# Gradient of a gated MLP beside an FFT convolution: gradient-row products queued behind the convolution's VectorE operation, one more idle slot ahead of the paired tiles, convolution stores held during four-bank products

## The chip, the core and the metric

The kernel runs on one core of a Trainium2 chip, in bf16 with f32 accumulation in PSUM. The metric is the device time of one execution in microseconds (us). Three runs of the kernel before gave 1858.02, 1858.46 and 1858.56, so the median is 1858.46. A profile was taken of one more execution. Its own time is 1857.48, and the span between its first and last recorded instruction is 1855.7; every time on the trace's axis counts from the start of that span.

## The reference

What has to be computed is the forward output and the nine gradients of

```python
xn = _layernorm(x, axis=-1)                      # x = A_q, [1, 2048, 1024]
return x + _A_ref(xn, A_k, A_v, shift_k, ssm_k, ssm_D) + _B_ref(xn, W_gate, W_up, W_down)
# A: kv = shift4(k) * v ; y = fftconv(kv, ssm_k) + kv * ssm_D ; result xn * y
# B: gate = xn @ W_gate ; up = xn @ W_up ; h = gate * (gate > 0) * up ; result h @ W_down
_out, _vjp = jax.vjp(_f, A_q, A_k, A_v, A_shift_k, A_ssm_k, A_ssm_D, B_W_gate, B_W_up, B_W_down)
```

with 2048 rows, 1024 columns and a hidden width of 3584. B_x is not used. So there is an MLP with three weight matrices, and its backward pass, and a long convolution with its backward pass.

## The kernel before, in words

**The MLP's phases.** Class LnMlp issues the large products, all of them as matmuls of 128x128 weights against 512 columns, eight to a group (`gemm8`) or sixteen (`gemm16`). `hidden` (L1121, 0 to about 631 us) has 14 blocks of 8 row tiles. A block does for each row tile a gate group (PSUM tile ps_g), an up group (ps_u) and a gradient-row group (ps_h, `grad_row`, L1301). ScalarE (ACT) evicts ps_h as gh (L1305), and VectorE (DVE) multiplies the row's pair ru by gh in place (L1306). VectorE also makes ru's second half out of ps_u (L1177) and the product ht (L1183). The stores of ht and ru (L1190, L1311) go to DRAM scratch h_d and ug_d; `defer` and `tick` issue them two steps late. `grad_down` (L1445, to about 846 us, ps_d) and `grad_in` (L1484, to 1272 us, ps_w) make the weight gradients. Both have a form called `four` (L1405) which works on four PSUM banks at once while its operands still arrive: once at the start and once at the end of `grad_down`, and once at the start of `grad_in`. The row tiles xn_nat are loaded (L1092) during the second of these, through its callback `freed`, and its successor uses them at L1413. `out_phase` (L1532, 1272 to 1460 us, ps_o) makes h @ W_down, and `grad_x` (L1648, ps_x) the gradient of x.

**The convolution.** Class ABranch does the FFT as small matmuls (PSUM tile ps_c, L83), evictions by ScalarE (L87), products and block transposes ("flips", `flip`, L341) on VectorE, for eight groups of 128 channels. It is a generator, `slots` (L691), which yields pairs: a block of matmuls or None, and a VectorE function or None. `steps` (L585) runs one pair at each turn: matmuls first, then the VectorE operation, then `stores` (L108), then at most one group of loads from a queue. A store is put on a list by `store` (L105) and issued by the third `stores` after it. The spectral product of a group begins with `f2_pair`, eight pieces that read what the flips of the last slots of the group before have written.

**Who sets the order.** The order on each engine is the program's own. The MLP's phases yield nanoseconds each time they have issued about eight matmuls (1730), and the loop at the end runs the convolution's next slot as soon as enough has gone by: 1900 for a slot with `hidden`; 1900 or, for a slot without matmuls, 1250 in the later phases, which are called dense. So a slot is a place between two groups of eight MLP matmuls, and what comes earlier in the code stands earlier in each engine's queue.

```python
    a_steps, left = a.steps(), A_START
            for ns in phase:
                left -= ns
                while a_steps is not None and left <= 0:
                    d = next(a_steps, None)
...
                        pri.strict = False
                        b.open_right(B_W_down)
                    else:
                        left += d
```

When the convolution has ended, its memory is released, the order is no longer held (`strict` is False; it became True when the convolution's slots began), and `open_right` (L1516) issues four loads of 1.75 MB each (L1522), which bring W_down for `out_phase` as tile wd: rows kt 0 to 6, 7 to 13, 14 to 20 and 21 to 27. They stand on the queue of SyncE (SP), which issues nearly all DMAs, in its program order. wd lies where convolution buffers lay, so its first load waits for their last reader, the store of gh to gh_d.

While `four` runs, `cap` is 2 instead of 3: the convolution may then use two PSUM banks in a block, and larger blocks are split into parts (`parts`, L545) that run one after the other.

Of the kernel before, what the change touches and what calls it, by code (L numbers as in the profile page):

```python
# [48 lines left out]
class ABranch:  # L49
# [58 lines left out]
    def stores(self):  # L108
        for o in self.out:
            o[0] -= 1  # L110
        while self.out and self.out[0][0] <= 0:
            _, out, in_ = self.out.pop(0)
            self.pri.late()
            self.pri.pin(self.nc.sync.dma_start(out=out, in_=in_))
# [576 lines left out]
    def slots(self, st, gi):  # L691
# [148 lines left out]
        yield None, flG  # L840
        yield None, None
        yield None, None

A_START = 60_000


class LnMlp:
# [273 lines left out]
    def hidden(self, first, goT, load, ln, tables, Wg, Wu, Wd, g, xn_d, h_d, ug_d):  # L1121
# [6 lines left out]
        for n in range(N):  # L1128
# [135 lines left out]
            def last_rows(sp):  # L1264

                self.hold = True
                for q in range(2):
                    load_down(sp // 2 + q)

                def run(f, s):  # L1270
                    f(s)
                    yield from step(self.PACE[f is up])
                yield from run(gate, sp)
                yield from run(gate, sp + 1)
                yield from run(up, sp)
                yield from run(gate, sp + 2)
                yield from run(gate, sp + 3)
                load_gate()
                yield from run(up, sp + 1)
                yield from grad_row(sp)  # L1280
                yield from run(up, sp + 2)
                yield from run(up, sp + 3)
                load_up()
                if n == 1:
                    chunk()
                if swap:
                    next_rows(sp)
                    next_rows(sp + 2)
                for s in range(sp + 1, HS):
                    yield from grad_row(s)  # L1290
                if swap:
                    next_grads(sp)
                    next_grads(sp + 2)
# [7 lines left out]
            def grad_row(s, after={}):  # L1301
                ps = self.ps_tile("ps_h")
                self.gemm8(ps, gT[s], wd, None, after)
                gh = self.e1_tile("gh")
                self.pri.pin(nc.scalar.copy(out=gh[:], in_=ps[:]))  # L1305
                self.pri.pin(nc.vector.tensor_tensor(out=ru[s][:], in0=ru[s][:], in1=gh[:].rearrange(  # L1306
                    "p (o f) -> p o f", o=1).to_broadcast([P, 2, 512]), op=ALU.mult))

                def store(r=(s0 + s) * P, cols=cols, t=ru[s]):
                    queue = nc.gpsimd if n == 0 and s < 2 else nc.sync  # L1310
                    self.pri.pin(queue.dma_start(out=ug_d[r:r + P, :, cols], in_=t[:]))  # L1311
                self.defer(store)
                yield 1730
                self.tick()

            def next_grads(sp):
# [6 lines left out]
            def grad(sp):  # L1323
                for s in (sp, sp + 1):
                    at = 3 if sp == 0 else 0
                    yield from grad_row(s, {at: lambda: flip_ahead(sp)} if ahead and s == sp + 1 else {})
                if swap:
                    next_grads(sp)
# [512 lines left out]
```

## Time and profile before

| | |
|---|---|
| median of three runs | 1858.46 us |
| profiled execution: its time, its span | 1857.48, 1855.7 us |
| instructions recorded | 32102 |
| VectorE, ScalarE, GpSimd busy | 60%, 35%, 1% of the span |
| TensorE matmuls in ps_w, ps_d (L1397) | 381.1 and 169.8 us, 379 ns each |
| convolution evictions (L87, 128x512) | 576, 293.9 us, 611 ns each |
| flips (L341) | 96, 180.3 us, 1933 ns each |
| DMA | 344.64 MB, mean 186 GB/s |
| granted TensorE clock | 9 of 10 or more in all 40 slices; 1.00 for the core |

PE is TensorE's matmuls, PEld its weight loads, DVE VectorE, ACT ScalarE, POOL GpSimd, SP SyncE and SPq SyncE's queue of DMA issues. Matmuls are pipelined: one of 512 columns shows 379 ns, but the next one starts about 216 ns after it. So the distance from start to start, rather than the busy time, tells where TensorE lost time. In a timeline a row is its start, the time to its end, the engine, the line, the operation, out<-in, the count, and in brackets the idle time just before it with what ended it. In a table of waits the three numbers are the total, the number of times and the longest.

### The profile page before, as it was taken

The numbers are of one execution on the slowest core, as the hardware profiler recorded it, in microseconds if no ns is written. First come the engines' busy times: TensorE is split into PE (matmuls) and PEld (weight loads), VectorE is DVE, ScalarE is ACT, GpSimd is POOL, SyncE is SP. The second block draws the span as 40 slices with busy tenths as digits, with TensorE's granted clock in tenths as the row PEclk, the third lists the DMA queues.
The fourth block names the chain that finished last, engine by engine and source line by source line (L and its number), as shares of the span: only waits on it lengthen the run. The fifth ranks groups of instructions, "written<-read, shape, count | busy, mean of one in ns | idle before, by whom it ended". The sixth has DMA issues, their size and how long they took to land.

```text
span 1855.7 us, 32102 instructions
## 1 busy us (share of the span) xinstructions
PE 1848.7 (100%) x13061; PEld 847.5 (46%) x13061; DVE 1114.7 (60%) x1634; ACT 646.4 (35%) x1215; POOL 22.6 (1%) x59
## 2 busy tenths in 40 slices
PE   9999999999999999999999999999999999999999
PEld 4444444444444444444444444444444544444444
DVE  6646797797789758584786676721122222466652
ACT  5644444544444454544545555330000000111100
POOL 1000000000000000000000000000000000000000
PEclk9999999999999999999999999999999999999999
DMA  9897669968757856549657444469999857799973
GB/s 269 243 215 191 155 174 235 223 153 205 173 156 197 254 158 165 140 123 257 150 138 177 134 136 126 139 176 292 238 252 250 195 144 166 175 209 212 200 159 74
DMA packets 747876, 344.64 MB, mean 186 GB/s; under 512 B 575832, under 2 KB 715088, under 8 KB 747728
## 3 DMA queue, kind: packets, MB, share of 16 engines
q1 hardware_dynamic: 736592, 320.30, 71.9%
q10 hardware_dynamic: 9504, 17.04, 3.1%
q0 software_dynamic: 1632, 5.24, 0.8%
q8 instruction: 102, 1.67, 0.4%
q14 instruction: 46, 0.38, 0.1%
HBM read 143.79 MB, written 103.83 MB: 133 GB/s over the span
## 4 chain that ended last, share of the span: by engine, by line
PE 71%; DVE 2%; DMA 1%; SPq 0%; issue 0%; DVEq 0%
PE ps_x L1693 21%; PE ps_w L1397 20%; PE ps_o L1561 10%; PE ps_d L1397 8%; PE ps_c L83 3%; PE ps_u L1062 2%; PE ps_h L1062 2%; PE ps_g L1062 2%; PE ps_d L1413 1%; DVE t L91 1%; PE ps_r L1595 0%; PE ps_w L1413 0%; DMA xn_nat<-xn_d 0%; DMA vt<-in_A_v_dram 0%; DVE u L91 0%; DVE arena L91 0%
## 5 line engine op out<-in xcount | busy, mean ns | idle before, releaser
L1397 PE MATMUL ps_w<-ugs,xn_nat 128*128 128x512 bf16 x1728 | 381.1, 379 | 0.0
L87 ACT CAST arena<-ps_c 128x512 bf16<-128x512 f32 x576 | 293.9, 611 | 82.5 <-PE ps_c L83 82.3
L1062 PEld LDWEIGHTS <-xnT 128*128 128x128 bf16 x1792 | 171.8, 98 | 208.8 <-issue 5.4
L341 DVE STREAM_TRANSPOSE arena<-arena 128x1024 f32<-128x1024 f32 x96 | 180.3, 1933 | 135.5 <-ACT arena L87 114.3
L1397 PEld LDWEIGHTS <-xn_nat 128*128 128x128 bf16 x1728 | 165.3, 98 | 201.1 <-issue 6.7
L1062 PE MATMUL ps_u<-wu,xnT 128*128 128x512 bf16 x896 | 206.0, 379 | 0.0
L1062 PE MATMUL ps_g<-wg,xnT 128*128 128x512 bf16 x896 | 205.2, 379 | 0.4 <-DVE xnT L1106 0.3
L1062 PE MATMUL ps_h<-wdT,goT 128*128 128x512 bf16 x896 | 204.1, 379 | 0.0
L1693 PE MATMUL ps_x<-wgT,ggT 128*128 128x512 bf16 x896 | 198.6, 379 | 0.0
L1693 PE MATMUL ps_x<-wuT,guT 128*128 128x512 bf16 x896 | 198.6, 379 | 0.0
L1711 ACT ACTIVATE w<-xn,m 128x512 f32<-128x512 bf16 x32 | 24.3, 807 | 479.5 <-DVE m L1704 366.1
L1561 PE MATMUL ps_o<-wd,hT 128*128 128x512 bf16 (+1 forms) x896 | 187.6, 372 | 0.0
L1397 PE MATMUL ps_d<-g_nat,hs 128*128 128x512 bf16 x768 | 169.8, 379 | 0.0
L1305 ACT CAST gh<-ps_h 128x512 bf16<-128x512 f32 x112 | 66.2, 591 | 201.6 <-PE ps_h L1062 188.8
L1693 PEld LDWEIGHTS <-guT 128*128 128x128 bf16 x896 | 87.7, 98 | 105.7
L1693 PEld LDWEIGHTS <-ggT 128*128 128x128 bf16 x896 | 87.7, 98 | 105.5
L1062 PEld LDWEIGHTS <-goT 128*128 128x128 bf16 x896 | 86.5, 98 | 104.1 <-issue 1.4
L1561 PEld LDWEIGHTS <-hT 128*128 128x128 bf16 x896 | 87.7, 98 | 100.0
L1400 ACT CAST wi<-ps_w 128x512 bf16<-128x512 f32 x108 | 64.6, 599 | 189.0 <-PE ps_w L1397 151.9
L1177 DVE SCALAR_TENSOR_TENSOR ru<-ru,ps_u 128x512 bf16<-128x512 bf16 x112 | 76.4, 683 | 83.6 <-PE ps_u L1062 43.2
L1553 DVE TENSOR_TENSOR ya<-ya,xe 128x1024 bf16<-128x1024 bf16 x16 | 11.1, 693 | 173.2 <-DMA xe<-xn_d 173.2
L91 DVE TENSOR_TENSOR t<-arena 128x2048 bf16<-128x2048 bf16 x96 | 114.1, 1219 | 0.5
(145 smaller groups left out, 1401.9 us busy)
## 6 DMA issues: line engine op xcount, KB each, us to landing
ugs<-ug_d SPq DMA_DIRECT2D x112, 256.0 KB, 5.0
ug_d<-ru SPq DMA_DIRECT2D x110, 256.0 KB, 3.3
wg<-in_B_W_gate_dram SPq DMA_DIRECT2D x56, 256.0 KB, 4.3
wu<-in_B_W_up_dram SPq DMA_DIRECT2D x56, 256.0 KB, 4.7
hs<-h_d SPq DMA_DIRECT2D x56, 256.0 KB, 4.1
out_dram<-wi SPq DMA_DIRECT2D x56, 256.0 KB, 3.9
h_d<-ht SPq DMA_DIRECT2D x108, 128.0 KB, 1.9
gt<-in_grad_out_dram SPq DMA_DIRECT2D x32, 256.0 KB, 5.7
```

What stands on the lines that cost most here:

```text
L83: self.pri.pin(self.nc.tensor.matmul(out, lhsT=lhsT, rhs=rhs, start=start, stop=stop))
L87: self.pri.pin(self.nc.scalar.copy(out=out, in_=in_))
L91: self.pri.pin(self.nc.vector.tensor_tensor(out=out, in0=in0, in1=in1, op=op))
L341: self.pri.pin(self.nc.vector.transpose(out=df[:, c0:c0 + 32, :], in_=sf[:, c0:c0 + 32, :]))
L1062: self.pri.pin(self.nc.tensor.matmul(ps[:], lhsT=xT[:, kt * P:(kt + 1) * P], rhs=w(kt), start=(kt == 0), stop=(kt == self.DT - 1)), always ...
L1177: return self.pri.pin(nc.vector.scalar_tensor_tensor(out=ru[s][:, 1, :], in0=ru[s][:, 0, :], scalar=0.0, in1=ps[:], op0=ALU.is_gt, op1=ALU ...
L1305: self.pri.pin(nc.scalar.copy(out=gh[:], in_=ps[:]))
L1397: self.pri.pin(self.nc.tensor.matmul(ps[:], lhsT=lhsT(st), rhs=rhs(st), start=(st == 0), stop=(st == self.ST - 1)))
L1400: self.pri.pin(self.nc.scalar.copy(out=out, in_=ps[:]))
L1561: nc.tensor.matmul(ps, lhsT=hT[:, kt, :], rhs=self.wd[:, kt, oc], start=(kt == 0), stop=(kt == self.FT - 1))
L1693: nc.tensor.matmul(ps, lhsT=T[:, kt, :], rhs=W[:, kt, oc], start=(i == 0), stop=(i == n - 1))
L1711: nc.scalar.activation(out=w[:, oc], in_=xn[:, oc], func=ACT.Identity, scale=m[:, 7:8], bias=m[:, 6:7])
```

## The change

It has three parts. `stores` issues nothing while `cap` is 2, so what is due during a four-bank product is issued at the first slot after it. `slots` yields one idle pair more at the end of a group, if the phase is not dense; in this kernel that is after the first and the second group. `grad_row` yields, in the strict stretch, between the eviction of ps_h and VectorE's product, instead of after the deferred store; so the convolution's operation of that slot stands ahead of the product on VectorE's queue.

```diff
@@ -108,7 +108,7 @@
     def stores(self):
         for o in self.out:
             o[0] -= 1
-        while self.out and self.out[0][0] <= 0:
+        while self.out and self.out[0][0] <= 0 and self.cap == 3:
             _, out, in_ = self.out.pop(0)
             self.pri.late()
             self.pri.pin(self.nc.sync.dma_start(out=out, in_=in_))
@@ -840,6 +840,8 @@
         yield None, flG
         yield None, None
         yield None, None
+        if not self.dense:
+            yield None, None
 
 A_START = 60_000
 
@@ -1303,6 +1305,10 @@
                 self.gemm8(ps, gT[s], wd, None, after)
                 gh = self.e1_tile("gh")
                 self.pri.pin(nc.scalar.copy(out=gh[:], in_=ps[:]))
+                behind = self.pri.strict
+                if behind:
+                    yield 1730
+                    self.pri.now()
                 self.pri.pin(nc.vector.tensor_tensor(out=ru[s][:], in0=ru[s][:], in1=gh[:].rearrange(
                     "p (o f) -> p o f", o=1).to_broadcast([P, 2, 512]), op=ALU.mult))
 
@@ -1310,7 +1316,8 @@
                     queue = nc.gpsimd if n == 0 and s < 2 else nc.sync
                     self.pri.pin(queue.dma_start(out=ug_d[r:r + P, :, cols], in_=t[:]))
                 self.defer(store)
-                yield 1730
+                if not behind:
+                    yield 1730
                 self.tick()
 
             def next_grads(sp):
```

## The prediction

> **What bounds the kernel now.** I read the page's busy line first, then the table of TensorE's waits, and then the timelines of the places which that table names.
>
> ```profile
> PE 1848.7 (100%) x13061; PEld 847.5 (46%) x13061; DVE 1114.7 (60%) x1634; ACT 646.4 (35%) x1215; POOL 22.6 (1%) x59
> PE ps_warm L1117 <- POOL warm L1114: 1.5, 1, 1.5
> PE ps_c L83 <- DVE arena L341: 1.0, 1, 1.0
> PE ps_w L1413 <- DMA xn_nat<-xn_d: 0.8, 3, 0.3
> PE ps_g L1062 <- DVE xnT L1106: 0.3, 1, 0.3
> ```
>
> TensorE is the bound from end to end: 1848.7 of 1855.7 us. The number of its matmuls does not change, so the change can only save what TensorE waits. That is little: leaving out the warm-up, the waits named are 1.0, 0.8 and 0.3 us. 0.2% of this kernel, about what a measurement of it can tell from no change, is 3.7 us, which is more than all of these together. So the question is which of them go, and whether a new one comes. Times below are on the trace's axis of before.
>
> Two constants: 512-column matmuls start 0.216 us apart, and entering a convolution block costs about 0.10 us more (17 matmuls from 857.24 would end at 860.91, the block starts at 861.01).
>
> **Part 1, the two extra idle slots and the product's place: the wait of 1.0 us.** The timelines of VectorE and TensorE around it:
>
> ```profile
> 487.65 0.69 DVE L1306 TENSOR_TENSOR ru<-ru,gh 128x1024 bf16<-128x1024 bf16 x1 [1.20 <-ACT gh L1305]
> 488.26 1.93 DVE L341 STREAM_TRANSPOSE arena<-arena 128x1024 f32<-128x1024 f32 x1
> ...
> 496.31 1.91 DVE L341 STREAM_TRANSPOSE arena<-arena 128x1024 f32<-128x1024 f32 x1
> ...
> 495.41 1.89 PE L1062 MATMUL ps_g<-wg,xnT 128*128 128x512 bf16 x8
> 498.27 0.85 PE L83 MATMUL ps_c<-arena,FW 64*32 64x256 bf16 x48 [0.96 <-DVE arena L341]
> ```
>
> Four flips of about 1.93 us, with products between them, end at 498.22; the paired tiles' block starts at 498.27. After 8 matmuls from 495.41 it was due at 497.14 + 0.10, so it is 1.03 us late. Two edits answer it. The extra slot moves the block behind 8 more MLP matmuls (the order lists show 72 instead of 64 since the block that feeds the flips), 8 x 0.216 = 1.73 us, which alone exceeds 1.03. And the product that stood ahead of the first flip, and had waited 1.20 us for ScalarE, stands behind it, which lets the flip start up to 1.20 + 0.61 us sooner. **Gain 1.03 us**; the slot itself has no instruction and costs nothing here. At the end of the first group the same slot meets no wait and gives nothing.
>
> What the moved product costs: behind it in VectorE's queue is the next row's L1177, which frees a ps_u bank; behind it by buffer are ru's store to ug_d and ru's six buffers. Product and operation are neighbours in the queue, so what follows both is unmoved, unless the convolution's operation is ready later than the product was. In `hidden` such waits come to 0.7 us in all. The smallest margins of TensorE for a bank freed by VectorE are, after 141 us, where the reordering begins, 0.41 and 0.46 us (at 268.4 and 249.3 us). So the cost lies between nothing and 0.7 - 0.41 = 0.3 us, and below nothing cannot be, for TensorE has no other wait on VectorE there. I take 0, since from 141 us to the end of `hidden` its products wait 27.9 us for gh (26 times, longest 2.7), time into which the convolution's operation now falls.
>
> **Part 2, stores held during `four`: the waits of 0.8 us.** SyncE's timeline, and TensorE's:
>
> ```profile
> 837.90 0.43 SPq L114 DMA_DIRECT2D gks_d<-gks  x1
> 838.42 2.39 SPq L1092 DMA_DIRECT2D xn_nat<-xn_d  x3
> 840.86 1.52 SPq L99 DMA_DIRECT2D gks<-gks  x2
> 842.49 1.50 SPq L114 DMA_DIRECT2D out_dram<-gv  x2
> 844.03 3.63 SPq L99 DMA_DIRECT2D vt<-in_A_v_dram  x2
> 847.76 4.61 SPq L1092 DMA_DIRECT2D xn_nat<-xn_d  x8
> ...
> 855.92 0.39 PE L1413 MATMUL ps_w<-ugs,xn_nat 128*128 128x512 bf16 x1 [0.24 <-DMA xn_nat<-xn_d]
> 856.59 0.39 PE L1413 MATMUL ps_w<-ugs,xn_nat 128*128 128x512 bf16 x1 [0.28 <-DMA xn_nat<-xn_d]
> 857.24 3.84 PE L1413 MATMUL ps_w<-ugs,xn_nat 128*128 128x512 bf16 x17 [0.26 <-DMA xn_nat<-xn_d]
> ```
>
> The last eight xn_nat loads land from 852.49 to 857.19, 0.67 us apart, and TensorE wants one every 0.216. Start to start, its matmuls lose (855.92 - 855.51) + (0.67 - 0.22) + (0.65 - 0.22) = 1.29 us. The gks_d store and the two gv stores ahead of them take 0.52 + 1.54 = 2.06 us of SyncE's queue, start to start. In the order list all three stand behind the eight ugs loads. Eight loads 2.06 us earlier: the last lands at 855.13, and it was wanted, without the earlier stalls, at 857.24 - 1.29 = 855.95. **Gain 1.29 us**, with 0.8 us to spare. The buffers that they fill are read last at 845.9 by ps_d, before these issues too. What is queued behind the held stores (xt and gt loads) is not later, since SyncE's queue is only reordered; nothing writes gks or gv before about 885 us.
>
> In the first `four` the convolution's blocks move with the slots, and one is no longer split: rows of 0.71 (x64, at 644.10) and 0.34 us (x8, at 646.63) become one like 0.86 us (x71, at 764.98). That saves 0.71 + 0.34 - 0.86 = 0.19 and one entry of 0.10: **gain 0.29 us**.
>
> **Part 3, what is late next: wd.** The last convolution block now stands 8 matmuls, 1.73 us, later, and all that follows the convolution with it. SyncE's timeline at its end:
>
> ```profile
> 1247.37 0.58 SPq L114 DMA_DIRECT2D gh_d<-gh  x1
> 1250.84 0.39 SPq L1522 DMA_DIRECT2D wd<-in_B_W_down_dram  x1
> 1252.08 0.38 SPq L1510 DMA_DIRECT2D out_dram<-wi  x1
> 1252.51 0.64 SPq L1522 DMA_DIRECT2D wd<-in_B_W_down_dram  x1
> ...
> 1266.31 0.47 SPq L1522 DMA_DIRECT2D wd<-in_B_W_down_dram  x1
> ...
> 1271.99 8.37 PE L1561 MATMUL ps_o<-wd,hT 128*128 128x512 bf16 x38
> ```
>
> wd's first load waits until gh_d has landed (1250.78). The hT transposes ahead of gh_d wait for TensorE (start 1230.70, then 1232.43), so gh_d lands between 1251.4 (SyncE's gaps take up the rest) and 1252.5. More important, the order list now puts a wi store, ready when ScalarE has evicted it (1252.06), ahead of the first wd load instead of behind it. So that load is issued at about 1252.08 + 0.42 = 1252.5, 1.66 us later. The DMA engines move almost nothing from 1250.3 to 1252.0 (5 and 9 GB/s in those slices) and are then full: the quarters land at 1259.14, 1264.51, 1269.84 and 1275.18, always 5.34 us apart, though the issues are 6.9 apart. So a later start moves the last landing one to one. By bytes the stream begins at 1251.95 now, and with the wi store's, 1.05 us after 1252.08, then: 1.15 us later. By issues it is 1.66.
>
> The fourth quarter's 1275.18 is for 15 of its 16 engines; the last comes at 1276.37, after a 16 KB instruction fetch of 1.12 us on that engine. TensorE wants it at the 22nd matmul, 1276.53. The margin is 0.16 us (the third quarter has 5.2). So TensorE waits 1.15 - 0.16 = **0.99 us** by bytes, 1.50 by issues, up to 0.6 more because the row loads of ya, xe and xr, from 1273.5, share the engines with the tail for longer, and nothing if the fetch falls elsewhere (1275.18 + 1.15 = 1276.33). I take the value by bytes and half of the sharing, 1.3 us; both ends, 0 and 2.1, stay in the range.
>
> The sum: 1857.48 - 1.03 - 1.29 - 0.29 + 1.3 = 1856.17 for an execution like the profiled one. The median of three is 0.98 above that execution, so I predict **1857.2 us**.
>
> On wd's rate the trace gives 2.10 MB (a quarter and a wi store) each 5.34 us, 393 GB/s. The Trainium skill, "DMA: Bandwidth & Descriptors", section "Specifications", limits a core to about 358 GB/s from HBM. By that a quarter would take an estimated 5.9 us and the fourth land some 2 us later than it does even before; the trace is against it.
>
> **The rivals.** *wd is hidden* (no late fetch, or the first load goes ahead sooner): for it speaks that 15 of 16 engines would be in time; against it the fixed place of the wi store. Full gain: 1857.48 - 2.61 + 0.98 = 1855.9. *wd costs more than is gained* (the other side): the stream slips not by 1.15 but by one more hT transposition, 4.14 us, as SyncE serves them one by one and a wi store is now ahead of the first. Then the wait is 4.14 - 0.16 = 3.98 and the time 1857.48 - 2.61 + 3.98 + 0.98 = 1859.8. It decides from a slip of 2.77 us, and would pass 0.2% only at 6.5. For it speaks that the chain SyncE, gh_d, wd has no slack; against it that the wi store ahead of hT is ready at 1252.06 - 3 x 6.9 = 1231.4, before hT may start. *The reordering does not help, or brings a new wait in `hidden`*: 1.03 not gained, 1858.2; for it speak only the small bank margins, against it that the extra slot alone is enough.
>
> The trace shows full clock (1.00) through waits of up to 0.96 us. The Trainium skill, "TensorE: Matmul & The Clock Gate", section "Part 1: The HAM clock gate", says that an idle window of about 3.4 us halves the clock until another busy one has passed; no run here shows it. By that page the second rival would cost an estimated 1.7 us more.
>
> **How the numbers follow.** Forecast 0.50, wd hidden 0.24, wd costing more 0.18, no help from the reordering 0.08. The range takes in the first three with the scatter of the runs (0.5): 1855.4 to 1860.3. Faster by over 0.2% (under 1854.7) needs a gain for which there is no wait left: 0.03. Slower by over 0.2% (over 1862.2) needs the large slip twice over: 0.07. Within 0.2%: 0.90.
>
> **What would show it.** No wait of the paired tiles' block near 500 us, and none on xn_nat; 128 convolution blocks instead of 129; the first wd load behind a wi store; a new wait of ps_o on wd of about 1.3 us, at the 22nd matmul. Wrong would be: an xn_nat wait that stays, new waits on L1177, or no wait on wd.

## The result, and the profile after

The changed kernel takes 1863.59 us (median of 8 runs, 1860.45 to 1865.85), the kernel before 1858.51 in the same runs (8 runs, 1857.31 to 1860.66). The ratio is 1.0026, with an interval of 1.0015 to 1.0037. So it is slower, by about 5 us, where the text on record says 1857.2 and a range up to 1860.3.

The page's busy line and the table of TensorE's waits of the changed kernel; code lines from 843 on stand 2 higher there, and from 1306 on 6 or 7:

```profile
PE 1850.7 (99%) x13061; PEld 847.8 (46%) x13061; DVE 1114.6 (60%) x1634; ACT 646.5 (35%) x1215; POOL 22.6 (1%) x59
PE ps_o L1568 <- DMA wd<-in_B_W_down_dram: 4.2, 1, 4.2
PE ps_warm L1119 <- POOL warm L1116: 1.5, 1, 1.5
PE ps_h L1064 <- ACT ru L1172: 0.6, 1, 0.6
PE ps_u L1064 <- DMA wu<-in_B_W_up_dram: 0.5, 1, 0.5
PE pst_x L1103 <- DVE ln_x L963: 0.5, 1, 0.5
PE ps_g L1064 <- DVE xnT L1108: 0.3, 1, 0.3
```

Both waits that the change was forecast to end are gone: no ps_c on a flip, no ps_w on xn_nat. In their place stands one wait of 4.2 us on wd, which was forecast at 1.3, and two in `hidden` of 0.6 and 0.5 us. The convolution now has 128 blocks instead of 129, as forecast.

The paired tiles' block near 500 us and the place where the xn_nat waits were, in TensorE's timeline:

```profile
500.63 3.62 PE L1064 MATMUL ps_u<-wu,xnT 128*128 128x512 bf16 x16
504.18 0.85 PE L83 MATMUL ps_c<-arena,FW 64*32 64x256 bf16 x48
...
854.66 5.57 PE L1420 MATMUL ps_w<-ugs,xn_nat 128*128 128x512 bf16 x25
```

SyncE's timeline ahead of the second place:

```profile
844.46 5.92 SPq L1094 DMA_DIRECT2D xn_nat<-xn_d  x8
850.48 0.86 SPq L1487 DMA_DIRECT2D out_dram<-wo  x2
851.53 6.11 SPq L1386 DMA_DIRECT2D ugs<-ug_d  x8
857.99 0.36 SPq L114 DMA_DIRECT2D gks_d<-gks  x1
858.81 2.01 SPq L114 DMA_DIRECT2D out_dram<-gv  x2
```

No bracket stands behind the block's row: 16 matmuls from 500.63 end at 504.08, and it starts 0.10 us later, the cost of any entry. The 25 matmuls on xn_nat run through without a gap. The held stores stand behind the ugs loads.

The tail, in SyncE's timeline:

```profile
1239.95 0.53 SPq L1517 DMA_DIRECT2D out_dram<-wi  x1
1240.52 5.44 SPq L1534 DMA_TRANSPOSE hT<-h_d  x1
1246.41 0.64 SPq L114 DMA_DIRECT2D out_dram<-gk  x1
1247.15 0.60 SPq L1517 DMA_DIRECT2D out_dram<-wi  x1
1247.81 1.33 SPq L114 DMA_DIRECT2D out_dram<-gk  x1
1249.18 0.82 SPq L114 DMA_DIRECT2D out_dram<-gh  x1
1250.05 1.02 SPq L114 DMA_DIRECT2D gh_d<-gh  x1
1251.24 0.38 SPq L1517 DMA_DIRECT2D out_dram<-wi  x1
1254.16 1.00 SPq L1529 DMA_DIRECT2D wd<-in_B_W_down_dram  x2
```

In TensorE's:

```profile
1271.15 5.34 PE L1568 MATMUL ps_o<-wd,hT 128*128 128x512 bf16 x24
1280.71 19.55 PE L1568 MATMUL ps_o<-wd,hT 128*128 128x512 bf16 x78 [4.21 <-DMA wd<-in_B_W_down_dram]
```

And in windows of 5 us (the window and its length, busy us of PE, PEld, DVE, ACT and POOL, each with its instructions, then granted clock, DMA share and GB/s):

```profile
1275.00:1280.00 5.00, 1.50 (x7) 0.58 (x6) 0.69 (x1) 0.00 (x0) 0.00 (x0) 0.91 0.90 330
1280.00:1285.00 5.00, 4.29 (x11) 1.53 (x11) 1.38 (x2) 0.00 (x0) 0.00 (x0) 0.50 0.48 104
1285.00:1290.00 5.00, 5.00 (x23) 2.19 (x22) 0.00 (x0) 0.00 (x0) 0.00 (x0) 0.91 1.10 223
```

The windows show a second loss that no table of waits has: behind the wait the granted clock is 0.50, and only 11 matmuls run in 5 us. Start to start, TensorE loses 4.38 us in the wait, and then 13 intervals of up to 0.427 instead of 0.216 us cost 2.54 more.

The wait of ps_h in `hidden`, in the timelines of ScalarE and TensorE (ps_h takes a PSUM bank that the relu of L1172 has to free):

```profile
351.84 0.60 ACT L1172 ACTIVATE ru<-ps_g 128x512 bf16<-128x512 f32 x1 [3.70 <-DMA ug_d<-ru]
352.48 0.81 PE L1064 MATMUL ps_h<-wdT,goT 128*128 128x512 bf16 x3 [0.64 <-ACT ru L1172]
```

The balance of the two profiled executions, whose spans differ by 6.1 us: 4.38 + 2.54 at wd, 0.80 + 0.71 in `hidden`, 0.17 in the first 10 us (no part of the change is there; that start varies from one execution to the next), 0.09 in a convolution block at 142 us, less 1.03 + 1.29 + 0.29 gained, is 6.1.

### The profile page after: what moved, and what is told of

Read it like the earlier page. It is cut to its first block, busy times and chain, and to the rows that moved or that the text cites. A ratio compares the mean times of both kernels' runs of the same rounds, so it can differ in the third digit from the quotient of the medians.

```text
span 1861.8 us, 32089 instructions
## 1 busy us (share of the span) xinstructions
PE 1850.7 (99%) x13061; PEld 847.8 (46%) x13061; DVE 1114.6 (60%) x1634; ACT 646.5 (35%) x1215; POOL 22.6 (1%) x59
## 4 chain that ended last, share of the span: by engine, by line
PE 98%; DMA 2%; ACT 0%; DVE 0%; issue 0%; ACTq 0%; SPq 0%; DVEq 0%
PE ps_x L1700 21%; PE ps_w L1404 20%; PE ps_h L1064 10%; PE ps_u L1064 10%; PE ps_g L1064 10%; PE ps_o L1568 10%; PE ps_d L1404 9%; PE ps_c L83 4%; PE ps_d L1420 2%; DMA wd<-in_B_W_down_dram 1%; PE ps_w L1420 1%; PE ps_r L1602 0%; DMA wu<-in_B_W_up_dram 0%; DMA ug_d<-ru 0%; DMA ln_x<-in_A_q_dram 0%; PE pst_x L1103 0%
```

## The experiments

Theory 1: the extra slots make the convolution's tail later, wd comes too late, and the long wait halves TensorE's clock. Theory 2: the moved product costs, through waits in `hidden`. Theory 3: the held stores cost. The kernel before was run again in each set of runs; its medians there are 1858.6 to 1858.9, and each ratio is against the one of its own set.

**Each part alone.** The first run holds the stores and nothing else.

```diff
-        while self.out and self.out[0][0] <= 0:
+        while self.out and self.out[0][0] <= 0 and self.cap == 3:
```

> Only the held stores. Theory 1 (the loss comes from wd, which the extra slots make late): the waits on xn_nat go, 1.3 us, and nothing else moves, so about 1857.2 beside 1858.5, no wait of ps_o on wd over 0.5 us, clock 1.00. Theory 2 (the loss comes from the moved product, through new waits in hidden): the same as theory 1 here. Theory 3 (the loss comes from the stores that are held, which collide later): slower by several us.

Measured: 1856.71, ratio 0.9992 (0.9983 to 1.0000). No wait on xn_nat, the paired tiles' wait of 1.0 stays, none on wd, clock 1.00. As theories 1 and 2 have it; theory 3 falls.

The second run has only the extra slots.

```diff
         yield None, None
+        if not self.dense:
+            yield None, None
```

> Only the two extra slots. Theory 1: the wait of the paired tiles goes (1.03) and the split block joins (0.29), but the tail of the convolution is 8 matmuls later as in the changed kernel: a wait on wd of about 4.2 us and a clock that is halved for about 11 matmuls behind it (2.4 us), so about +5.5 us, 1864.0. Theory 2: no such wait, about 1857.2. Theory 3: as theory 2.

Measured: 1865.53, ratio 1.0032 (1.0023 to 1.0041). TensorE's waits in `hidden` and later, without its own issue:

```profile
PE ps_o L1563 <- DMA wd<-in_B_W_down_dram: 5.0, 1, 5.0
...
PE ps_u L1064 <- DMA wu<-in_B_W_up_dram: 0.9, 1, 0.9
PE ps_h L1064 <- ACT ru L1172: 0.9, 1, 0.9
PE ps_w L1415 <- DMA xn_nat<-xn_d: 0.5, 2, 0.3
```

The slots alone make the whole loss. The ten executions fall in two kinds: 1859.42 and 1861.17 with a mean granted clock of 1.000, and eight from 1864.21 to 1866.89 with 0.998 or 0.999. The paired tiles' wait is gone here too, with the product where it was. Theory 2 falls as the cause. The wait of ps_h, which theory 2 wanted to put down to the moved product, is here without it.

The third run has only the moved product (the edit of `grad_row` in the change).

> Only the product behind the convolution's operation. Theory 1: the tail is that of before, so no wait on wd; the wait of the paired tiles shrinks from 1.03 to nothing or little, and up to 0.8 us of new waits in hidden (ps_h behind a relu that waits for ru's store) come: between -1.0 and +0.8 us, 1857.5 to 1859.3. Theory 2: the loss is here, the new waits come to 1.5 us or more, 1860 or more. Theory 3: about 1857.5.

Measured: 1857.31, ratio 0.9992 (0.9983 to 1.0001), 0.2 below theory 1's range and far from the 1860 of theory 2. TensorE's timeline:

```profile
496.02 1.89 PE L1062 MATMUL ps_g<-wg,xnT 128*128 128x512 bf16 x8
497.84 0.85 PE L83 MATMUL ps_c<-arena,FW 64*32 64x256 bf16 x48
```

The paired tiles' block stands 1.73 + 0.09 us behind the start of the 8 matmuls: the wait is gone without any extra slot. No wait of ps_h on a relu; one on wu of 0.4 us. Theory 1 holds.

The fourth run is the change without its slots, that is, the first and the third together.

> The change without its extra slots (held stores and moved product together). Theory 1: the sum of the two runs that do these alone, with the tail of before: -2.3 to -0.5 us, 1856.2 to 1858.0, no wait on wd. Theory 2: at least +0.2 us, 1858.7 or more. Theory 3: slower by several us.

Measured: 1857.28, ratio 0.9994 (0.9985 to 1.0003), inside theory 1's bounds, below theory 2's and theory 3's. Neither the paired tiles nor xn_nat are waited for, nor wd. One of its eleven executions took 1861.88, with a mean granted clock of 0.998, and one of the 32 of the kernel before 1863.30, with 0.999. Neither was profiled; that wd came late there too, now and then, without any slot, is likely but not shown.

**The tail put back.** The change whole, but with one idle slot of the last group skipped, which gives the convolution's last block and SyncE's order around wd back.

```diff
         yield None, tg
-        yield None, None
+        if not last:
+            yield None, None
         fly = self.flip_C(self.Cy, 0)
```

> The change whole, but the last group skips one idle slot (the one behind its fourth tap product), so that the convolution's last block and SyncE's order around wd are again those of before. Theory 1 (the extra slots cost only through the tail): no wait on wd, the other gains kept, 2.6 us less up to 1.5 us of new waits in hidden: 1856.0 to 1857.5. Rival (the slots cost where they stand, in hidden and behind it): stays at 1860 or more.

Measured: 1856.71, ratio 0.9992 (0.9983 to 1.0001); ten of eleven executions under 1857.2, one at 1861.88. TensorE's timeline has no wait on wd:

```profile
1271.61 18.72 PE L1569 MATMUL ps_o<-wd,hT 128*128 128x512 bf16 x84
```

So what the slots cost beyond `hidden` goes through the tail alone. In `hidden` they cost: this run's profile has the wait of ps_h on the relu with 1.3 us.

**Sharing the DMA engines.** The change whole, but the row loads of the first row tile of `out_phase` stand behind wd on SyncE's queue (`wd_in` is wd's last load).

```diff
...
+            if st:
+                for t, src in ((ya, y_d), (xe, xn_d), (xr, x)):
+                    tc.keep_in_program_order(nc.scalar.dma_start(out=t[:], in_=src[rows, :]))
+            else:
+                with tc.issue_after(self.wd_in.ins):
+                    for t, src in ((ya, y_d), (xe, xn_d), (xr, x)):
+                        nc.sync.dma_start(out=t[:], in_=src[rows, :])
```

> The change whole, but the three row loads of the first row tile of the output phase (ya, xe, xr, 0.79 MB) stand on SyncE's queue behind wd's last load instead of on ScalarE's beside it. If sharing the DMA engines with them makes wd's last quarter late, as theory 1 now has it, the wait on wd falls by about 2.0 us (0.79 MB at 393 GB/s) from 4.2 to about 2.2, below what slows the clock, so another 2.4 us go: about 1859.3. Rival (the stream only starts too late, sharing is nothing): the wait stays at 4 us and the time at 1863.6.

Measured: 1859.35, ratio 1.0007 (0.9998 to 1.0016), as forecast; two of the eleven executions took over 1863. Its TensorE timeline:

```profile
1279.24 10.95 PE L1570 MATMUL ps_o<-wd,hT 128*128 128x512 bf16 x49 [1.88 <-DMA wd<-in_B_W_down_dram]
```

And its window behind the wait:

```profile
1280.00:1285.00 5.00, 4.95 (x24) 2.25 (x23) 2.08 (x3) 0.00 (x0) 0.00 (x0) 1.00 0.88 199
```

The wait is 1.9 instead of 4.2 us, and behind it 24 matmuls run in 5 us at full clock. Sharing costs some 2.3 us, and with it the clock.

**The clock by itself.** The kernel before, with a copy between two scratch places in DRAM ahead of wd's last quarter, of 0.5 and of 1.57 MB (256 rows, as printed, and 768). wd's loads are kept in program order too, so that the copy stands ahead of the last one.

```diff
         for a in range(0, self.FT, 7):
...
+            if a == 21:
+                self.tc.keep_in_program_order(self.nc.sync.dma_start(out=self.more[:], in_=Wd[0:256, :]))
+            self.tc.keep_in_program_order(self.nc.sync.dma_start(
+                out=self.wd[:, a:a + 7, :], in_=Wd[a * P:(a + 7) * P, :].rearrange("(kt p) o -> p kt o", p=P)))
```

> The kernel before, with a copy of 0.5 MB from one scratch place in DRAM to another, which nothing reads, on SyncE's queue ahead of wd's last quarter. At 393 GB/s it makes that quarter 1.34 us later; with 0.16 us of margin and 0.6 to 1.3 us for sharing with the row loads the wait on wd is 1.8 to 2.5 us. Theory of the clock (only an idle time of more than about 3.4 us halves it): clock 1.00 and 1860.3 to 1861.0. Rival (any wait of this size slows the clock): 1862.7 or more.

Measured: 1858.66, ratio 1.0004 (0.9995 to 1.0013), below what was expected: by their times most executions did not wait as long as that. The profiled one (1860.30) waited longer than the 1.8 to 2.5 us expected, and serves for the clock: 3.09 us lost, start to start, and full clock behind it.

> As the run with the copy of 0.5 MB, but 1.57 MB: 4.0 us later, a wait on wd of 4.4 to 5.2 us. Theory of the clock: behind the wait the matmuls start 0.427 us apart for about 11 of them, 2.4 us more, so 1865.3 to 1866.1. Rival (the wait is all of the cost): 1862.9 to 1863.7.

Measured: 1865.48 (four executions), ratio 1.0038 (1.0024 to 1.0052), inside the range of the theory of the clock. The window behind the wait, with the copy of 0.5 MB:

```profile
1280.00:1285.00 5.00, 5.00 (x24) 2.25 (x23) 1.82 (x3) 0.00 (x0) 0.00 (x0) 1.00 0.52 116
```

With 1.57 MB, TensorE's timeline and then the same window:

```profile
1281.77 18.53 PE L1563 MATMUL ps_o<-wd,hT 128*128 128x512 bf16 x74 [4.89 <-DMA wd<-in_B_W_down_dram]
```

```profile
1280.00:1285.00 5.00, 3.23 (x8) 1.16 (x8) 1.43 (x3) 0.00 (x0) 0.00 (x0) 0.50 0.31 83
```

An idle time of 3.09 us leaves the clock as it is; one of 5.05 us halves it and costs 2.18 us more. With no part of the change in the kernel, this is the changed kernel's loss made by hand.

The length of the wait is not all that counts. Two windows inside the changed kernel's wait, of 1 us each:

```profile
1278.50:1279.50 1.00, 0.00 (x0) 0.00 (x0) 0.29 (x1) 0.00 (x0) 0.00 (x0) 0.79 0.72 259
1279.50:1280.50 1.00, 0.00 (x0) 0.00 (x0) 0.40 (x1) 0.00 (x0) 0.00 (x0) 0.50 0.12 41
```

The clock is halved while TensorE still waits, at 1279.08 by the trace's record of the granted clock, 2.6 us after the last matmul's end. In the runs with only the slots and with 1.57 MB that is 3.0 and 2.5 us after it. In all three the half clock lasts 6.83 us, and what of it lies behind the restart (5.20, 4.80, 4.45 us) costs 2.54, 2.35, 2.18 us. In every trace of this case the time from one change of the clock to the next is a whole multiple of 3.41 us, so changes come on a fixed grid. In the thirteen traces a step of that grid at full clock with 0.9 us of matmuls or less is always followed by the half clock, and one with 1.4 us or more never. The step that the wait leaves emptiest holds 0.83 us in the changed kernel, 0.89 with 1.57 MB and 1.41 with 0.5 MB. So, as an estimate (3.41 - 0.9), a wait somewhat over 2.5 us can halve the clock if it lies badly on the grid; no run here shows one that did.

**Why wd is so late.** In the changed kernel the first gk store of the last group stands behind the three transpositions, and was ahead of them before. Here the last group's two gk stores count one slot less, which puts the first back; the last block stays late, and a wi store stays ahead of wd.

```diff
         self.store_time(self.out_gk, st["cg"], gk)
+        for o in self.out[-2:]:
+            o[0] -= 1 * last
```

> The change whole, but the last group's two gk stores count one slot less before they are issued, which puts the first of them ahead of the three hT transpositions again, as before the change; the wi store stays ahead of wd and the last block stays 8 matmuls late. Theory: wd's first load is 4.2 us late because the order on SyncE lets the third transposition and the stores behind it run slow (5.4 instead of 4.1 us), 2.5 us of it from there and 1.7 from the later block. Then the transposition takes about 4.1 us, the first wd load is 1.7 us late, the wait on wd falls from 4.2 to 1.7 to 2.0 us, the clock stays at 1.00: about 1859.0. Rival (the later block alone makes all of the lateness): wait of 3.5 us or more, 1862 or more.

Measured: 1858.10, ratio 0.9997 (0.9988 to 1.0006), lower than the 1859.0 expected and far from the rival's 1862. SyncE's timeline:

```profile
1229.12 0.60 SPq L114 DMA_DIRECT2D out_dram<-gk  x1
1230.66 8.43 SPq L1536 DMA_TRANSPOSE hT<-h_d  x2
1239.20 0.52 SPq L1519 DMA_DIRECT2D out_dram<-wi  x1
1239.76 5.15 SPq L1536 DMA_TRANSPOSE hT<-h_d  x1
...
1248.53 0.58 SPq L114 DMA_DIRECT2D gh_d<-gh  x1
1250.32 0.38 SPq L1519 DMA_DIRECT2D out_dram<-wi  x1
1252.20 1.00 SPq L1531 DMA_DIRECT2D wd<-in_B_W_down_dram  x2
```

TensorE's:

```profile
1277.68 12.68 PE L1570 MATMUL ps_o<-wd,hT 128*128 128x512 bf16 x58 [2.11 <-DMA wd<-in_B_W_down_dram]
```

The wait halves, to 2.1 us, at full clock, so the place of the gk store is about half of the wait. But the theory's reason is wrong in part: the third transposition still takes 5.15 us, where 4.1 was expected, and wd's first load is 3.1 us late, where 1.7 was expected (1252.20 + 1.76 against 1250.84; `out_phase` starts 1.76 sooner here than in the kernel before).

**What beats both kernels.** The change with the slot taken back and the row loads behind wd:

> The change whole with the last group's idle slot taken out and with the first row tile's row loads behind wd: both repairs together. If the runs of the repaired tail still lose now and then to a late last engine on wd (its highest time was 1861.9), the row loads out of the way should lower that: median 1856.4 to 1856.7, no time over 1860. Rival (that scatter comes from elsewhere, the program's first 10 us or hidden): the same median and the same highest times.

Measured: 1857.04, ratio 0.9995 (0.9986 to 1.0003); the highest time is 1860.13, where none over 1860 was expected. No gain can be told from the version without the row loads moved, and the rival is not excluded.

Held stores and moved product, no slots, row loads behind wd:

> Held stores and moved product without extra slots, with the row loads behind wd. If the extra slots bring the new wait of ps_h at 351 us (0.8 to 1.5 us in each run that has them, none in those without), this is the fastest version: 1855.8 to 1856.5, no such wait. Rival (it is no faster than the version with slots, since the paired tiles' wait comes back in part): 1856.7 or more.

Measured: 1856.33, ratio 0.9990 (0.9981 to 0.9999), the lowest median, though the intervals do not tell it from the other repaired versions. In its profile TensorE's only waits on another engine or a DMA are in the program's first 12 us:

```profile
PE ps_warm L1117 <- POOL warm L1114: 1.5, 1, 1.5
PE pst_x L1101 <- DVE ln_x L961: 0.9, 1, 0.9
PE ps_g L1062 <- DVE xnT L1106: 0.3, 1, 0.3
```

## Why the prediction was wrong, point by point

**What bounds the kernel, and what can be gained:** right. The gains forecast come to 2.6 us, and the best version is 2.6 us (0.14%) below the kernel before, in the medians of its runs (0.2 to 3.5 by the interval).

**Part 1, the paired tiles:** the gain was right (the wait is gone), and each of the two edits ends it alone, the slot in the second run and the product in the third. But that the slot "costs nothing here" was wrong. The profiles of the six versions that have the slots in `hidden` all show ps_h waiting behind a relu (0.80 us in the changed kernel, 0.84 to 1.50 in the other five, all at 351 to 354 us); in four of them the trace names a store of ru as what the relu waited for, in the other two a matmul. The profiles of the four with the parts but without slots show no such wait. What the moved product costs, taken as 0, is open: a wait on wu at 278 us (0.5 to 1.1 us) is in six of the nine profiles that have the slots in `hidden` or the moved product, and in none of the four that have neither, so no single part can be named for it. The third run, with the product alone, is no slower for it.

**Part 2, held stores:** right. The first run has the whole of it by itself. The split block that becomes one is the slots' doing, not the stores': with the held stores alone it stays split.

**Part 3, wd:** that TensorE would wait for wd was right. What makes wd late was wrong, and the terms of the sum were too small.
- The step "gh_d lands between 1251.4 (SyncE's gaps take up the rest) and 1252.5" failed. It landed at 1254.10, and since the changed kernel's TensorE is 0.84 us ahead there (1271.15 against 1271.99), that is 1254.9 on the axis of before. The sum counted the first transposition's start (1232.43, which came true: 1231.59 + 0.84), but took the stores behind it to be as quick as before. The third transposition took 5.44 instead of 4.14 us, and the gk store that the order list shows behind it came in too.
- "More important, the order list now puts a wi store ... ahead of the first wd load" failed with it: that store was issued at 1251.24, and wd waited 2.5 us longer for gh_d. So wd's first load was issued 4.2 us later (1254.16 + 0.84 against 1250.84), not 1.66, and the last landing moved by 5.1 us (1280.67 + 0.84 against 1276.37), not by 1.15.
- "TensorE wants it at the 22nd matmul" did not hold for the changed kernel: 24 matmuls run ahead of the wait, and the first half of the columns ends at the 31st instead of the 28th. Three matmuls of the second half stand ahead of the one that needs the last quarter, which took 0.65 us off the wait: 5.14 - 0.16 - 0.65 = 4.33, where 4.38 was measured.
- Sharing with the row loads was put at up to 0.6 us, and the run with these loads behind wd shows about 2.3. The estimate counted only the added overlap. But a quarter that is later lies beside all 0.79 MB of them.
- The clock was in no term. The rival "wd costs more than is gained" had a wait of 3.98 us, close to the 4.38 measured, and priced it at 1859.8, since a wait was taken to cost its own length. The half clock is 2.54 us on top, and with the 1.5 us in `hidden` that makes about the time measured. That its wait came so close is luck: its reason, one more transposition of 4.14 us ahead of wd, is not in the trace, where three transpositions stand there as before.

The Trainium skill, "TensorE: Matmul & The Clock Gate", section "Part 1: The HAM clock gate", was cited for an idle window of about 3.4 us. By the lengths of the waits the runs agree: full clock after 2.04, 2.27 and 3.09 us lost, half after 4.38, 5.05 and 5.15. But the clock was halved 2.5 to 3.0 us after the last matmul's end, so less than 3.4 us of idle time was enough. The extra cost estimated from that page was 1.7 us, and 2.18 to 2.54 were measured.

The chance of the rival that came nearest was 0.18, and its price set the end of the range at 1860.3. A range that held the clock's loss would have ended above 1862.

**What stays open:** why the third transposition is slower. It takes 5.15 to 5.81 us in the four versions whose last block is late, and 3.93 to 4.46 in all the others. During it the DMA engines of the changed kernel move almost nothing for about 1.5 us, and a 16 KB instruction fetch falls there, which in the others comes after the transposition's issue. That the fetch does it was not tested.

## What to carry to other kernels

A slot that is empty is not free: it makes all that follows later, and has to be followed to the last thing that the moved work releases, here a 7 MB load with 0.16 us of margin. When a later start is summed, each row behind it must be taken again in its new order, on its queue and on the DMA engines that it shares. A wait on TensorE that may reach 3 us or more should be priced with a half clock behind it, here 2.2 to 2.5 us on top (not seen up to 3.09 us lost, seen from 4.38 on; between them no run lies); and of three edits that go together, each should be tried alone, for here one of them alone made the loss, and the two others made the gain without it.

## What the runs showed of the hardware

- TensorE's clock in a wait: full after 3.09 us lost, half in waits of 4.38 us and more, from 2.5 to 3.0 us after the last matmul's end and for 6.83 us; 11 to 13 matmuls of 512 columns behind the wait were slower (2.18 to 2.54 us lost). Its changes lie whole multiples of 3.41 us apart.
- Where TensorE at full clock was busy for 0.9 us or less of such a step of 3.41 us, the clock was halved at the step's end, in all thirteen traces; where it was busy for 1.4 us or more, it stayed full.
- The sixteen engines' parts of one load can land far apart: wd's last quarter from 1277.65 to 1280.67 in the changed kernel, beside row loads on another queue, and from 1277.63 to 1279.20 with these loads behind it. TensorE waits for the last.
- Transposing loads of 0.92 MB each hold SyncE's queue for 3.6 to 5.8 us, and the stores behind them land 3.8 to 5.0 us after their issue in the changed kernel, the one of 0.2 KB (gh) as late as the rest.
